# Second chunk of tokens: its second layer in split half precision instead of plain fp32, the weight splits and one batch's key preparation in other places

## Chip, cores, metric

One core of one Trainium2 chip. The metric is the device time of the program in microseconds (us); the time before is the median of three runs.

## What is computed

Attention over 4 batches, 8 heads, 576 positions and 64 columns per head, in which each row keeps only its 32 largest scores, and then two feed-forward layers over the 2304 tokens that come out.

```python
def _attn_ref(q, k, v):
    top_k = 32
    scores = scale * np.matmul(q, k.transpose(0, 1, 3, 2))
    kth = np.partition(scores, -top_k, axis=-1)[..., -top_k:-top_k + 1]
    scores = np.where(scores >= kth, scores, -1000000000.0)
    ...
    return np.matmul(attn, v).astype(np.float32)

def _moe_ref(x, w_gate, w_val, w_out):        # 512 -> 1536 -> 512
    gate = 1.0 / (1.0 + np.exp(-(x @ w_gate)))
    return (gate * (x @ w_val) @ w_out).astype(np.float32)

def _moe2_ref(x, w_in, w_out):                # 512 -> 2048 -> 512
    r = np.maximum(x @ w_in, 0.0)
    return (r * r @ w_out).astype(np.float32)
```

## The kernel before

**Tiles and chunks.** The 2304 tokens are 18 tiles of 128. They go through the kernel in 12 chunks: chunks 0 to 5 have one tile, chunks 6 to 11 two. For every chunk attention is computed first, in blocks: one block is one tile and one head, 128 rows by 576 scores. Chunks 0 to 5 have 8 blocks each (numbers 0 to 47 here), the others 16 each, 144 in all. In names a block is written as tile and head: `mx_2_1` is tile 2, head 1, which is block 17. A block takes, on VectorE (DVE), four `MAX8` (L389) and three `MATCH_REPLACE8` (L396) to find the 32nd largest score; ScalarE (ACT) copies scores out of PSUM and does the exponentials (L377, L408, L424), GpSimd (POOL) scales, TensorE (PE) multiplies queries by keys (`sp`, L374), turns the weights (`tp`, `tq`) and multiplies by the values (`xp`). Blocks go strictly one after the other on DVE, so the number of the block is the clock of the attention.

**The layers.** After a chunk's blocks come its two layers: `pg` and `pv` (gate and value, 6 pairs of column blocks), `acc1` (first layer's output), `ph` (8 pairs) and `acc2`. `th` (L759; `g`, L917, in the plain form) is the DVE product of gate and value that `acc1` waits for. There are two forms:

- **plain** (`moe32`, chunks 0 and 1): fp32 weights (`wg_c`, `wv_c`, `wo_c`, `wi_c`, `w2_c`) and fp32 activations.
- **split** (`moe`, chunks 2 to 11): weights and activations each as the sum of two fp16 numbers, high and low, and three fp16 products (`SPLIT`) for one fp32 product. The activations between the layers get a power-of-two scale from a sum of squares (`x2pq`, `x2cm`, `x2s`).

**The weights** come as 8-byte numbers through SyncE's queue (SP, L580). `conv` makes fp32 of them (ACT L607, L613, L616; DVE L609, L620; POOL L623); 34 pairs of blocks. `scale` finds a power-of-two scale for each weight matrix from its Gram matrix on PE (L640). `split` then makes the two fp16 parts of a pair: ACT L658 and DVE L661, or, for every third pair, POOL L663 and L664 in place of DVE. A pair's fp32 form can be given up only when the last plain chunk that needs it is through; the fp16 parts go into slots of the same pool of 35.

**Keys** of a batch are turned and cut into two parts by `prep_keys`, for two heads at a time: three loads (L152, L154), five PE transposes (L165), ACT copies (L172), DVE differences (L173), and four stores to DRAM (L179), which the loads `kst` (L326) read back. Batch 1 is first used in chunk 4.

**Order.** Program order on each engine is made before the run by a scheduler that walks the code with priorities. The loop at the end of the kernel sets them: in the plain part it gives attention blocks, conversion steps and layer steps due times (`ta`, `tw`, `tm`, with the steps `CA`, `CA2`, `CW`, `CM`), and `todo` holds the splits with the layer step after which each may come. From chunk 2 on, `attend` keeps attention a fixed number of blocks (`LEAD`, `LEAD2`) ahead of the layers. At run time each engine, SP's queue too, works through its own list strictly in that order.

Of the kernel before, what the change touches and what calls it, by code (L numbers as in the profile page):

```python
# [74 lines left out]
def tile_topk_attention__then__two_moe_layers(  # L75
# [692 lines left out]
    def moe(ci, nxt=None):  # L768

        m = ahead.pop(ci)  # L770
        tts, N, ix, l1_pair = chunks[ci], m.N, m.ix, m.l1_pair
        accs = []

        def l1_acc(fp, gh):
            if not accs:
                for h in range(2):
                    accs.append(ps_a.tile([P, 512], F32, tag="acc", name=f"acc1_{ci}_{h}"))

            last = fp == NF1 // 2 - 1
            for e, d in sorted(  # L780
                ((e, d) for e in range(2) for d in range(KM)),
                key=lambda t: (t[1], t[0]) if last else t,
            ):
                f = 2 * fp + e
                if True:
                    for x, (a, b_) in enumerate(SPLIT):
                        nc.tensor.matmul(  # L787
                            accs[d // 2][:, (d % 2) * N : (d % 2 + 1) * N],
                            wblk("wo", a, f, d * P, P),
                            gh[:, b_, e * N : (e + 1) * N],  # L790
                            start=(f == 0 and x == 0 and d % 2 == 0),
                            stop=(f == NF1 - 1 and x == 2),
                            skip_group_check=True,
                        )

        queue = m.queue
        depth = max(1, len(queue))
        for fp in range(len(queue), NF1 // 2):
            queue.append((fp, l1_pair(fp)))
            yield  # L800
            if len(queue) > depth:
                l1_acc(*queue.pop(0))
        while len(queue) > 1:
            l1_acc(*queue.pop(0))
        if nxt:
            nxt()
        l1_acc(*queue.pop(0))

        pool, kw = (wpool, {"tag": "w"}) if ci >= X2W else (mpool, {"tag": "m4", "bufs": M4})
        x2 = pool.tile([P, 2, KM, N], F16, name=f"x2_{ci}", **kw)  # L810
# [472 lines left out]
```

## Time and profile before

| | before |
|---|---|
| median of three runs (lowest to highest) | 1272.48 us (1272.18 to 1277.38) |
| profiled execution, its own time / its span | 1270.1 us / 1267.8 us |
| busy: PE, DVE, ACT, POOL | 1171.9, 956.3, 830.0, 844.9 us |
| share of the span | 92%, 75%, 65%, 67% |
| mean granted clock of TensorE | 0.966 |

The span runs from the first to the last instruction. Busy time is what the profiler saw each engine work; the rest of the span is idle time. The granted clock is the share of full speed that TensorE was allowed.

### The profile page before, as it was taken

What the parts mean: (1) busy time and instruction counts of PE and PEld (TensorE: products, weight loads), DVE (VectorE), ACT (ScalarE), POOL (GpSimd) and SP (SyncE); (2) the same over time, 40 slices, a digit from 0 to 9 for tenths busy, and PEclk for the clock granted to TensorE, in tenths of its full rate; (3) what the DMA queues carried; (4) which work ended last, traced back from release to release, by engine and by line L of the source; (5) the groups of instructions that cost most, each with busy time, mean ns of one, the idle gap of its engine ahead of it and who ended that gap; (6) DMA issues with size and microseconds to landing.
All of it is one profiled execution on the core that took longest, in us unless ns stands there. A gap on an engine that the chain in (4) does not pass through costs nothing.

```text
span 1267.8 us, 30670 instructions
## 1 busy us (share of the span) xinstructions
PE 1171.9 (92%) x11477; PEld 952.5 (75%) x11477; DVE 956.3 (75%) x1965; ACT 830.0 (65%) x1719; POOL 844.9 (67%) x1294
## 2 busy tenths in 40 slices
PE   6657889999889989899998999999999999999998
PEld 5436877987777868779786778877886887787775
DVE  6998789899789868889997788998999969210010
ACT  4998996577676766667766676776676757322122
POOL 1788774488776576777875887797688749515223
PEclk9667999999989999999997999999999999999999
DMA  6988763223354346665667465466544623200000
GB/s 183 366 293 284 259 191 85 57 78 88 109 151 118 95 93 147 147 134 119 146 128 155 99 164 120 119 138 154 105 101 92 126 48 67 55 1 1 18 1 17
DMA packets 243188, 153.92 MB, mean 121 GB/s; under 512 B 193120, under 2 KB 209504, under 8 KB 243040
## 3 DMA queue, kind: packets, MB, share of 16 engines
q1 hardware_dynamic: 243040, 151.97, 47.1%
q8 instruction: 90, 1.47, 0.5%
q14 instruction: 58, 0.48, 0.1%
HBM read 105.51 MB, written 18.09 MB: 97 GB/s over the span
## 4 chain that ended last, share of the span: by engine, by line
PE 62%; DVE 14%; ACT 9%; DMA 7%; POOL 5%; issue 3%; SPq 1%; DVEq 0%; POOLq 0%; ACTq 0%
PE ph L851 11%; PE acc L872 10%; PE pv L747 7%; PE pg L747 7%; PE acc L787 6%; PE sp L374 6%; DVE mx L389 5%; DVE W L396 5%; PE xp L506 2%; PE ph L952 2%; DMA PT<-S 2%; DMA kst<-ks 2%; PE acc L969 2%; PE xp L533 2%; PE qpt L334 1%
## 5 line engine op out<-in xcount | busy, mean ns | idle before, releaser
L389 DVE MAX8 mx<-W 128x8 f32<-128x576 f32 x432 | 327.9, 759 | 11.1
L396 DVE MATCH_REPLACE8 W<-mx,W 128x576 f32<-128x576 f32 x288 | 213.8, 742 | 0.0
L851 PE MATMUL ph<-x,wi_w 128*128 128x256 f16 (+1 forms) x1920 | 190.7, 252 | 4.6 <-ACT x L825 3.6
L872 PE MATMUL acc<-w_w,rh 128*128 128x512 f16 x768 | 181.8, 379 | 2.2 <-POOL rh L864 2.2
L851 PEld LDWEIGHTS <-wi_w 128*128 128x128 f16 x1920 | 156.4, 98 | 30.6 <-issue 5.2
L747 PE MATMUL pv<-xs,wv_w 128*128 128x256 f16 (+1 forms) x1440 | 147.0, 254 | 6.0 <-DVE th L759 4.8
L747 PE MATMUL pg<-xs,wg_w 128*128 128x256 f16 (+1 forms) x1440 | 148.2, 253 | 3.1 <-ACT xs L520 2.2
L374 PE MATMUL sp<-kst,qt 128*128 128x288 f32 x608 | 135.3, 335 | 15.7 <-DMA kst<-ks 8.8
L408 ACT ACTIVATE W<-S,mx 128x576 f32<-128x576 f32 x144 | 111.8, 776 | 51.7 <-DVE mx L389 51.4
L454 POOL TENSOR_TENSOR S<-W,S 128x512 f16<-128x512 f32 x192 | 137.0, 736 | 1.6
L747 PEld LDWEIGHTS <-wv_w 128*128 128x128 f16 x1440 | 117.9, 99 | 22.1 <-issue 9.2
L747 PEld LDWEIGHTS <-wg_w 128*128 128x128 f16 x1440 | 118.6, 99 | 17.4 <-issue 1.0
L377 ACT COPY S<-sp 128x576 f32<-128x576 f32 x144 | 92.0, 639 | 57.3 <-PE sp L374 37.5
L872 PEld LDWEIGHTS <-rh 128*128 128x128 f16 x768 | 72.5, 98 | 74.0 <-POOL rh L864 2.8
L787 PEld LDWEIGHTS <-wo_w 128*128 128x128 f16 x1440 | 117.9, 98 | 12.6 <-issue 0.8
L389 DVE MAX8 mx<-S 128x8 f32<-128x576 f32 x144 | 107.3, 745 | 25.0 <-ACT S L377 25.0
L759 DVE TENSOR_TENSOR th<-pv,th 128x512 f32<-128x512 f32 (+1 forms) x60 | 34.5, 576 | 121.3 <-PE pv L747 113.9
L374 PEld LDWEIGHTS sp<-kst,qt 128*128 128x128 f32 x608 | 92.4, 196 | 27.8 <-DMA kst<-ks 8.0
L452 POOL TENSOR_SCALAR W<-W,rz 128x576 f32<-128x576 f32 x96 | 71.9, 749 | 59.8 <-ACT S L451 57.4
L863 POOL TENSOR_TENSOR r<-r 128x512 f32<-128x512 f32 (+1 forms) x80 | 69.6, 871 | 57.4 <-ACT rh L862 51.8
L451 ACT ACTIVATE S<-W,rz 128x576 f16<-128x576 f32 x96 | 74.2, 774 | 50.4 <-DVE rz L447 47.1
L396 DVE MATCH_REPLACE8 W<-mx,S 128x576 f32<-128x576 f32 x144 | 106.9, 743 | 0.3 <-issue 0.3
(290 smaller groups left out, 2349.6 us busy)
## 6 DMA issues: line engine op xcount, KB each, us to landing
kst<-ks SPq DMA_DIRECT2D x112, 288.0 KB, 3.2
v<-vd SPq DMA_DIRECT2D x32, 320.0 KB, 3.4
qn<-in_q_dram SPq DMA_DIRECT2D x128, 64.0 KB, 2.4
wi_r<-in_moe_w_in_dram SPq DMA_DIRECT2D x16, 512.0 KB, 6.1
w_r<-in_moe_w_out_dram SPq DMA_DIRECT2D x16, 512.0 KB, 4.5
v<-in_v_dram SPq DMA_DIRECT2D x56, 128.0 KB, 2.4
wg_r<-in_moe_w_gate_dram SPq DMA_DIRECT2D x12, 512.0 KB, 6.4
wv_r<-in_moe_w_val_dram SPq DMA_DIRECT2D x12, 512.0 KB, 7.0
```

The lines of the kernel that those rows point to most:

```text
L374: nc.tensor.matmul(sp[:, e, 0:HALF], l, r, start=(x == 0), stop=(x == len(ops) - 1))
L377: nc.scalar.copy(ss.rearrange("p (e s) -> p e s", e=2), sp[:, :, 0:HALF])
L389: m8 = nc.vector.max(mx[:, r], cur)
L396: nc.vector.match_replace(wk, mx[:, r], cur, NEG)
L408: nc.scalar.activation(wk, ss, AF.Prelu, bias=kth, scale=-1.0, alpha=1.0 / BIG)
L451: nc.scalar.activation(pp[:, 0:S], wk, AF.Copy, scale=rz)
L452: nc.gpsimd.tensor_scalar(wk, wk, rz, 1.0, op0=ALU.mult, op1=ALU.mult)
L454: nc.gpsimd.tensor_tensor(pp[:, o : o + e - f], wk[:, f:e], pp[:, f:e], op=ALU.subtract)
L747: nc.tensor.matmul(pp[:, e * N : (e + 1) * N], wblk(wd, a, c, f0, P), xs[:, b_, c, :], start=(e == 0 and n == 0), stop=(n == 3 * KM - 1), ...
L787: nc.tensor.matmul(accs[d // 2][:, (d % 2) * N : (d % 2 + 1) * N], wblk("wo", a, f, d * P, P), gh[:, b_, e * N : (e + 1) * N], start=(f == ...
L851: nc.tensor.matmul(ph[:, e * N : (e + 1) * N], wblk("wi", a, c, f0, P), x2[:, b_, c, :], start=(e == 0 and n == 0), stop=(n == 3 * KM - 1) ...
L872: nc.tensor.matmul(acc2[i][:, 0:DM], gh[:, b_, e * N + i * P : e * N + (i + 1) * P], wblk("w2", a, f, 0, DM), start=(f == 0 and x == 0), s ...
```

## The change

Chunk 1 keeps its plain first layer, but its second layer is computed in the split form, by the same code as chunks 2 to 11 (moved out of `moe` into `second`). Since plain `wi` and `w2` are then last used in chunk 0, their splits come first: from the second half of chunk 0's steps on, with `wg`, `wv` and `wo` behind them during chunk 1. `wi` and `w2` get their Gram matrices at steps 7 and 11 in place of 9 and 13. Batch 1's keys are prepared during chunk 2's blocks (`KEYS1 = 2`), not chunk 1's. The plain form's `g` and `rr` are written over their inputs, and chunk 0's second layer keeps two pairs in flight, not one. Steps of chunk 1's second layer are set 3 apart in the due times, not 4.

```diff
-TD = 0
+MIXED = (1,)
+DEPTH1 = (1, 1)
+DEPTHP = 2
+CMS = 3.0
+W2S = 12
...
-KEYS1 = 1
-GRAM = {2: ("wg",), 3: ("wv",), 5: ("wo",), 9: ("wi",), 13: ("w2",)}
+KEYS1 = 2
+GRAM = {2: ("wg",), 3: ("wv",), 5: ("wo",), 7: ("wi",), 11: ("w2",)}
...
+    def second(ci, ix, x2, srcs, nxt=None):
+
+        tts = chunks[ci]
+        N = len(tts) * P
         KH = KM // 2
-        srcs = [a[:, 0 : KH * N].rearrange("p (d n) -> p d n", d=KH) for a in accs]
         with tc.high_priority(offset=XUP):
...
+        i2 = scales["w2"][1]
         us = mpool.tile([P, 2], F32, tag="us", bufs=2, name=f"us_{ci}")
-        nc.vector.scalar_tensor_tensor(us[:, 0:1], ix, iy, usc, op0=ALU.mult, op1=ALU.mult)
+        if ix is None:
+
+            nc.vector.scalar_tensor_tensor(
+                us[:, 0:1], iy, float(2.0 ** (2 * TB - 7)), scales["wi"][1], op0=ALU.mult, op1=ALU.mult
+            )
...
-            g = mpool.tile([P, 2 * N], F32, tag="hi", bufs=HIB, name=f"g_{ci}_{fp}")
-            nc.vector.tensor_tensor(g, pg[:, 2 * N : 4 * N], th, op=ALU.mult)
-            return g
+            nc.vector.tensor_tensor(th, pg[:, 2 * N : 4 * N], th, op=ALU.mult)
+            return th
...
+        if ci in MIXED:
+            x2 = xt.rearrange("p d n -> p (d n)").bitcast(F16)
+            h = KM * N // 2
+            yield from second(
+                ci,
+                None,
+                x2.rearrange("p (a c n) -> p a c n", a=2, c=KM),
+                [accs[0][:, i * h : (i + 1) * h].rearrange("p (d n) -> p d n", d=KM // 2) for i in range(2)],
+            )
+            return
...
+    ends = {n: (len(PLAIN) - 1) * per_chunk for n in ("wg", "wv", "wo")}
+    ends.update({n: (len(PLAIN) - 1 - len(MIXED)) * per_chunk for n in ("wi", "w2")})
     for i in range(len(pairs_of["wg"])):
-        todo.append((2 * (i // 2) + 2, "wg", i))
-        todo.append((2 * (i // 2) + 2, "wv", i))
+        todo.append((ends["wg"] + 2 * (i // 2) + 2, "wg", i))
+        todo.append((ends["wv"] + 2 * (i // 2) + 2, "wv", i))
...
-        todo.append((n1 + 2 * (i // 2) + 2, "wi", i))
+        todo.append((ends["wi"] + n1 + 2 * (i // 2) + 2, "wi", i))
     for i in range(len(pairs_of["w2"])):
-        todo.append((n1 + i + 3, "w2", i))
-    todo = [(max(t[0], TD), *t[1:]) for t in todo]
+        todo.append((ends["w2"] + max(n1 + i + 2 + DEPTHP, W2S), "w2", i))
...
-                tm += CM
-                if ci == PLAIN[-1]:
+                tm += CM if ci not in MIXED or n <= n1 else CMS
+                if nstep[0] == len(steps):
                     at(tm - SUP)
-                    while todo and todo[0][0] <= n:
+                    while todo and todo[0][0] <= PLAIN.index(ci) * per_chunk + n:
                         split(*todo.pop(0)[1:])
```

How the scheduler's lists move is seen at three places. (Lines of the changed kernel stand some 4 to 28 higher than in the kernel before.)

**SP's queue in chunk 1, before**, between two loads of keys for its heads 3 and 4 and the weight loads (`wi_r`):

```order
L326 DMA kst_1_3_0_994<-ks_0_1_145 128x576
L326 DMA kst_1_4_0_1082<-ks_0_2_245 128x576
L179 DMA ks_1_1_981<-kp_1_1_969 64x576 x2
L154 DMA ke_1_2_1350<-in_k_dram 64x2x64
L580 DMA wi_r2_2_1415<-in_moe2_w_in_dram 128x1024
L580 DMA wi_r3_2_1417<-in_moe2_w_in_dram 128x1024
L179 DMA ks_1_1_981<-kn_1_1_964 64x576 x2
L580 DMA wi_r0_3_1459<-in_moe2_w_in_dram 128x1024
```

The same place of the change, from the first of the two key loads:

```order
L330 DMA kst_1_3_0_949<-ks_0_1_145 128x576
L584 DMA wo_r4_0_748<-in_moe_w_out_dram 128x1024
L584 DMA wo_r5_0_750<-in_moe_w_out_dram 128x1024
L584 DMA wo_r6_0_808<-in_moe_w_out_dram 128x1024
L584 DMA wo_r7_0_810<-in_moe_w_out_dram 128x1024
L330 DMA kst_1_4_0_1036<-ks_0_2_245 128x576
L584 DMA wo_r8_0_822<-in_moe_w_out_dram 128x1024
```

Stores of batch 1's keys (`ks_1_1`), which wait for ACT and DVE, no longer stand ahead of weight loads; the queue has reached earlier weights (`wo_r`, not `wi_r`) when it comes to the keys of head 3.

**DVE in block 17, before** (tile 2, head 1): the scale of `wi` is worked out between the steps of the block.

```order
L389 MAX mx_2_1_2198<-S_2_1_2102 128x8
L646 TENSOR_TENSOR wi_d_2014<-wi_n_1948,ident_81 128x128
L396 MATCH_REPLACE W_2_1_2197<-mx_2_1_2198,S_2_1_2102 128x576
L389 MAX mx_2_1_2198<-W_2_1_2197 128x8
L429 RECIPROCAL rz_2_0_2151<-bs_2_0_2147 128x1
L396 MATCH_REPLACE W_2_1_2197<-mx_2_1_2198,W_2_1_2197 128x576
```

In the change (lines 4 higher) the same block holds the last conversion of `w2` and four splits of `wi`:

```order
L613 TENSOR_SCALAR w2_c7_1683<-w2_c7_1683 128x1024
L134 TENSOR_SCALAR wisn_1840<-wicx_1834 128x1
L137 TENSOR_SCALAR wis_1842<-wisn_1840 128x1
L140 TENSOR_SCALAR wis_1842<-wisn_1840 128x1
L1173 SCALAR_TENSOR_TENSOR usc_4630<-usc_4630,wis_1842 128x1
L665 SCALAR_TENSOR_TENSOR wi_w0_1857<-wi_c0_1026,wis_1842,wi_w0_1857 128x1024
L400 MATCH_REPLACE W_2_1_2245<-mx_2_1_2246,S_2_1_2036 128x576
L665 SCALAR_TENSOR_TENSOR wi_w1_1860<-wi_c1_1186,wis_1842,wi_w1_1860 128x1024
L393 MAX mx_2_1_2246<-W_2_1_2245 128x8
L400 MATCH_REPLACE W_2_1_2245<-mx_2_1_2246,W_2_1_2245 128x576
L665 SCALAR_TENSOR_TENSOR wi_w3_1949<-wi_c3_1349,wis_1842,wi_w3_1949 128x1024
```

Before, these `wi` splits stand in blocks 29 to 33.

**DVE in block 33, before** (tile 4, head 1), where the layers of chunk 2 run beside it (`th_2_2` is its product for pair 2):

```order
L661 SCALAR_TENSOR_TENSOR w2_w3_3263<-w2_c3_1707,w2s_2361,w2_w3_3263 128x1024
L396 MATCH_REPLACE W_4_1_3720<-mx_4_1_3721,S_4_1_3568 128x576
L389 MAX mx_4_1_3721<-W_4_1_3720 128x8
L661 SCALAR_TENSOR_TENSOR w2_w4_3330<-w2_c4_1719,w2s_2361,w2_w4_3330 128x1024
L396 MATCH_REPLACE W_4_1_3720<-mx_4_1_3721,W_4_1_3720 128x576
L759 TENSOR_TENSOR th_2_2_3970<-pv_2_2_3921,th_2_2_3970 128x256
```

The same block of the change:

```order
L400 MATCH_REPLACE W_4_1_3896<-mx_4_1_3897,S_4_1_3744 128x576
L393 MAX mx_4_1_3897<-W_4_1_3896 128x8
L400 MATCH_REPLACE W_4_1_3896<-mx_4_1_3897,W_4_1_3896 128x576
L393 MAX mx_4_1_3897<-W_4_1_3896 128x8
L763 TENSOR_TENSOR th_2_3_4227<-pv_2_3_4178,th_2_3_4227 128x256
L400 MATCH_REPLACE W_4_1_3896<-mx_4_1_3897,W_4_1_3896 128x576
```

The splits are gone from here, and chunk 2 is one pair further.

## Rows read from the trace of the kernel before

**Rows 1.** Stretches: us, busy PE, PEld, DVE, ACT, POOL, clock, DMA, GB/s.

```profile
84.30:193.50 109.20, 87.77 (x713) 76.10 (x714) 90.81 (x171) 99.83 (x180) 86.02 (x83) 0.87 0.76 246
193.50:252.50 59.00, 59.00 (x522) 50.52 (x521) 51.30 (x107) 34.13 (x72) 25.24 (x48) 1.00 0.25 70
252.50:314.20 61.70, 59.84 (x479) 50.10 (x477) 58.94 (x107) 48.54 (x94) 49.58 (x65) 1.00 0.30 83
314.20:388.60 74.40, 65.63 (x864) 58.41 (x862) 61.00 (x127) 53.84 (x127) 56.64 (x96) 0.93 0.45 126
388.60:435.90 47.30, 47.30 (x644) 40.99 (x641) 45.23 (x99) 33.66 (x80) 26.55 (x57) 1.00 0.36 98
435.90:563.70 127.80, 112.50 (x1520) 93.18 (x1518) 99.77 (x231) 86.50 (x211) 92.74 (x170) 1.00 0.58 131
563.70:1085.00 521.30, 510.34 (x5094) 407.42 (x5092) 467.59 (x979) 361.77 (x762) 400.85 (x663) 0.99 0.54 117
1085.00:1267.80 182.80, 176.40 (x1433) 135.94 (x1431) 12.67 (x28) 45.12 (x75) 59.88 (x64) 1.00 0.05 14
...
365.00:370.00 5.00, 4.27 (x27) 3.78 (x26) 4.93 (x13) 2.59 (x6) 3.78 (x8) 0.51 0.80 224
```

**Rows 2.** The same stages for L389 alone: us, DVE busy (instructions), clock, DMA.

```profile
193.50:252.50 59.00, 23.63 (x33) 1.00 0.25 70
563.70:1085.00 521.30, 236.30 (x321) 0.99 0.54 117
```

**Rows 3.** Chain that ended last, in order of time: start, us, what, records.

```profile
283.64 1.78 PE ph L952 x16
285.43 1.72 PE acc L969 x4
372.16 1.56 PE ph L851 x28
1156.80 2.59 PE acc L872 x12
```

**Rows 4.** Groups by form: line, names, shapes, count | busy us, mean ns | idle.

```profile
L661 DVE SCALAR_TENSOR_TENSOR w_w<-w_c,w2s,w_w 128x1024 f16<-128x1024 f32 x5 | 10.1, 2020 | 0.9 <-ACT w_w L658 0.9
L661 DVE SCALAR_TENSOR_TENSOR wi_w<-wi_c,wis,wi_w 128x1024 f16<-128x1024 f32 x6 | 8.6, 1435 | 0.1
L609 DVE TENSOR_SCALAR w_c<-w_c 128x1024 uint32<-128x1024 uint32 x8 | 6.6, 829 | 6.4 <-ACT w_c L607 6.4
L173 DVE TENSOR_TENSOR kn<-kpt,kp 128x512 fp32r<-128x512 f32 x12 | 8.2, 682 | 2.8 <-ACT kp L172 2.8
L172 ACT CAST kp<-kpt 128x512 fp32r<-128x512 f32 x16 | 9.5, 591 | 7.0 <-PE kpt L165 6.9
L607 ACT ACTIVATE w_c<-w_r 128x512 f32<-128x512 f32 x16 | 10.2, 677 | 0.4 <-POOL w_c L623 0.4
L826 DVE SCALAR_TENSOR_TENSOR x<-acc,x2s,x 128x256 f16<-128x256 f32 x8 | 3.6, 472 | 0.1
L864 POOL TENSOR_TENSOR rh<-r,rh 128x256 f16<-128x256 f32 x32 | 21.4, 673 | 0.7
```

**Rows 5.** Waits, SP 84 to 194 us, DVE 0 to 390: us, times, longest.

```profile
SPq L179 <- ACT kp L172: 8.8, 3, 5.6
...
DVE w_c L609 <- ACT w_c L607: 6.4, 3, 3.7
DVE wi_c L609 <- ACT wi_c L607: 6.3, 2, 4.4
```

**Rows 6.** Timeline of PE and DVE, 332 to 344 us.

```profile
332.10 1.50 PE L747 MATMUL pv<-xs,wv_w 128*128 128x128 f16 x24
332.85 4.37 DVE L661 SCALAR_TENSOR_TENSOR w_w<-w_c,w2s,w_w 128x1024 f16<-128x1024 f32 x1
341.04 2.57 PE L747 MATMUL pv<-xs,wv_w 128*128 128x128 f16 x24 [4.75 <-DVE th L759]
```

**Rows 7.** Chain that ended last, shares by line, 436 to 564 us.

```profile
by line: DMA PT<-S 13.7%; DVE mx L389 10.8%; DVE W L396 9.0%; DMA kst<-ks 8.2%; PE ph L851 7.9%; PE sp L374 5.7%; issue 5.0%; PE acc L872 4.9%; PE pg L747 3.3%; DMA vd<-vom 3.2%; PE pv L747 3.2%; PE acc L787 2.6%; SPq L298 2.5%; DMA kn<-in_
```

More of the change, by code (lines that the diff above doesn't have):

```diff
@@ L766, in moe_head @@
         m.N, m.ix, m.l1_pair = N, ix, l1_pair
[L768 to L810, printed above, removed]
+    def second(ci, ix, x2, srcs, nxt=None):
+        tts = chunks[ci]
+        N = len(tts) * P
         KH = KM // 2
-        srcs = [a[:, 0 : KH * N].rearrange("p (d n) -> p d n", d=KH) for a in accs]
         with tc.high_priority(offset=XUP):
@@ L892, in moe, with l1_acc @@
         yield
+    def moe(ci, nxt=None):
+        m = ahead.pop(ci)
+        tts, N, ix, l1_pair = chunks[ci], m.N, m.ix, m.l1_pair
+        accs = []
+        def l1_acc(fp, gh):
+            if not accs:
+                for h in range(2):
+                    accs.append(ps_a.tile([P, 512], F32, tag="acc", name=f"acc1_{ci}_{h}"))
+            last = fp == NF1 // 2 - 1
+            for e, d in sorted(
+                ((e, d) for e in range(2) for d in range(KM)),
+                key=lambda t: (t[1], t[0]) if last else t,
+            ):
+                f = 2 * fp + e
+                if True:
+                    for x, (a, b_) in enumerate(SPLIT):
+                        nc.tensor.matmul(
+                            accs[d // 2][:, (d % 2) * N : (d % 2 + 1) * N],
+                            wblk("wo", a, f, d * P, P),
+                            gh[:, b_, e * N : (e + 1) * N],
+                            start=(f == 0 and x == 0 and d % 2 == 0),
+                            stop=(f == NF1 - 1 and x == 2),
+                            skip_group_check=True,
+                        )
+        queue = m.queue
+        depth = max(1, len(queue))
+        for fp in range(len(queue), NF1 // 2):
+            queue.append((fp, l1_pair(fp)))
+            yield
+            if len(queue) > depth:
+                l1_acc(*queue.pop(0))
+        while len(queue) > 1:
+            l1_acc(*queue.pop(0))
+        if nxt:
+            nxt()
+        l1_acc(*queue.pop(0))
+        pool, kw = (wpool, {"tag": "w"}) if ci >= X2W else (mpool, {"tag": "m4", "bufs": M4})
+        x2 = pool.tile([P, 2, KM, N], F16, name=f"x2_{ci}", **kw)
+        KH = KM // 2
+        srcs = [a[:, 0 : KH * N].rearrange("p (d n) -> p d n", d=KH) for a in accs]
+        yield from second(ci, ix, x2, srcs, nxt)
     def moe32(ci, xt):
@@ L961, in l2_pair @@
             nc.scalar.activation(r, ph[:, 0 : 2 * N], AF.Relu)
-            g = mpool.tile([P, 2 * N], F32, tag="hi", bufs=HIB, name=f"rr_{ci}_{fp}")
-            nc.gpsimd.tensor_tensor(g, r, r, op=ALU.mult)
-            return g
+            nc.gpsimd.tensor_tensor(r, r, r, op=ALU.mult)
+            return r
         def l2_acc(fp, g):
@@ L975, in l2_acc @@
                 )
-        prev = None
+        prev = []
         for fp in range(NF2 // 2):
-            g = l2_pair(fp)
+            prev.append((fp, l2_pair(fp)))
             yield
-            if prev is not None:
-                l2_acc(*prev)
-            prev = (fp, g)
-        l2_acc(*prev)
+            if len(prev) > DEPTHP:
+                l2_acc(*prev.pop(0))
+        for p in prev:
+            l2_acc(*p)
         tt = chunks[ci][0]
@@ L1149, in layer2_scales @@
             usc.append(u)
-        return usc[0], scales["w2"][1]
+        return usc[0]
     att = attention()
```

19 lines of the change are left out of this document (11 added, 8 removed).

## Prediction

> **What bounds the kernel now.** I read first the table of stretches, cut where DVE begins blocks 8, 16, 24, 32, 40, 48, 64 and where its last block ends [rows 1]. The row of L389 shows that a cut is right: 33 `MAX8` in the second stretch are 8 blocks of 4, and one more at the edge [rows 2]. Four kinds of stage stand out. In blocks 8 to 15 ACT is busy 99.8 of 109.2 us: it converts weights. In blocks 16 to 31 PE is busy 118.8 of 120.7 us and DVE 110.2. In blocks 32 to 39 nobody is full (PE 65.6 of 74.4). In blocks 48 to 63 PE idles 15 us, and the chain of waits there runs through DMA (`PT`, `kst`) and DVE's L389 and L396, with little PE in it [rows 7]. After that PE is busy 98% until block 143 ends, and then 183 us of layers are left that PE does alone [rows 1]. So the end is set by how early the attention gets through the first 64 blocks, and from there on by PE's work.
>
> The profiled execution took 1270.1 us; the median of the runs is 2.4 above it. The sum is made against 1270.1, and 2.4 is added. A measurement of this kernel can tell some 0.5% from no change, 6.4 us.
>
> **What is removed and added.** Plain second layer of chunk 1: a `ph` pair is 16 records, 8 products at 0.222 each, in 1.78 us, an `acc` pair 4 records, 2 products at 0.86, in 1.72 [rows 3]; 8 of each, 28.0 us. In the split form it is 192 fp16 products of 128 columns at 1.56/28 = 0.056 us and 48 of 512 columns at 2.59/12 = 0.216 [rows 3], 10.7 + 10.4, and 4 for `x2pq`, 21.3. PE saves 6.7 us. DVE gets two halves of L826 at 0.47 [rows 4] and a handful of one-column steps, 2 us; POOL 8 operations of 0.67 [rows 4], 5.4, and ACT as many of about the same size. POOL and ACT are idle 12 and 13 of the 62 us of that stage [rows 1], which hides them; bare, in a chain of 8 pairs, they would cost up to 5.
>
> **What is moved.** I counted by the lists of both kernels what stands between the same blocks on DVE and PE, and priced it by rows. One price is open: a DVE split cost 2.02 us in the mean for `w2` and 1.44 for `wi` [rows 4]. I take 1.6, nearer the lower, since 6 against 5 splits are of it and the rest is between.
>
> *Blocks 0 to 15.* DVE loses 4 key preparations (0.68 and a short end each, 3.6 us), 4 conversion pairs of `w2` (0.83 and sign steps, 6 in all), 2 splits (3.2), one gate product: 13. PE loses 52 plain products at 0.222 and 2 at 0.86, 13 us, and 20 transposes, which I price like plain products, 4. ACT, which bounds this stage, loses 8 conversions at 0.68, 3 more of that size, 2 of twice the size, 4 key copies at 0.59 and their ends [rows 4], 2 splits: 15.8 in all. At its present share of 91%, 84.0 us of ACT take 92. That is -17 us. The least gain: DVE's 13 alone, less what it now waits, -10. The most: SP's stores waited 8.8 us for the key copies, with weight loads behind them in the queue, and DVE waited 12.7 us for conversions [rows 5]; half of that gone makes -24.
>
> *Blocks 16 to 23.* Here it is paid back. DVE gets 17 more splits (27), the 4 key preparations (3.6), 4 conversion pairs (6) and 3 gate products: 38 on top of 51.3, 89.3. PE gets 97 more plain products at 0.222, 2 at 0.86, and the transposes: 27 on top of 59.0, 86. DVE is the fuller one. In blocks 24 to 31, where both were full, it was busy 95.5% [rows 1]; at that share 89.3 us take 93.5: +34.5. The least loss: PE alone at its 97%, 88.7, +29.7. The most: all 20 splits at 2.02 and the conversions dearer too, +46.
>
> *Blocks 24 to 31.* 8 splits fewer, 2 us more for the new layer: DVE 58.9 becomes 47. PE: 130 plain products at 0.222 and 10 at 0.86 give way to 30, 202 fp16 ones at 0.056 and 42 at 0.216; 59.8 becomes 49.6, which at 97% take 51.1: -10.6. Between -12 and -6.
>
> *Blocks 32 to 39.* 7 splits leave. One of them took 4.37 us, the gate product `th` stood behind it on DVE, PE waited 4.75 us for `th`, and its next 24 products took 2.57 us where 24 before had taken 1.50 [rows 6]. The granted clock later fell to half once more (0.51 in 365 to 370) [rows 1]. The stage's mean clock of 0.93 means that some 10 of its 74.4 us ran at half (1.2 GHz); half of that, less what was idle, makes 4.5 of PE's 65.6 us. By count 5.2 us more of products come in. 66.3 us at 97% are 68.4: -6. Between -9 (no wait at all) and 0 (a wait of the same kind comes back elsewhere in the stage).
>
> *Blocks 40 to 47.* PE loses 3.4 of 47.3, but DVE gets 2 of chunk 3's layer work on 45.2; 47.5 at 95.5% are 49.8: +2.5 (-1 to +3).
>
> *Blocks 48 to 63.* PE has 3.9 us less. The chain there is little PE's [rows 7], so half comes through: -2 (0 to -4).
>
> *Blocks 64 on.* 4.5 us less for PE by count, at 98% busy: -4 (-2.5 to -4.5). After block 143 the lists hold the same work, 0.
>
> Sum: -17 + 34.5 - 10.6 - 6 + 2.5 - 2 - 4 = -2.6, so 1267.5, and 1270 as a median. The saved 6.7 us of PE are mostly given back as idle time of PE in the dense stage (93.5 against 86).
>
> **A rule against the change.** The two `w_w` and `wi_w` rows show the same DVE instruction at 2020 and 1435 ns [rows 4], and a single one at 4.37 us [rows 6]. The Trainium skill, SBUF — State Buffer, section "SBUF: two separate sides", says that DVE and GpSimd share one pair of ports by an exclusive lock, and that a DVE operation with two SBUF inputs and a GpSimd operation that reads SBUF keep each other out for a whole instruction. The two durations agree with it, though no row names the lock. By this rule 20 DVE splits in one stage, with POOL's own splits beside them, would nearly all pay the higher price; that is the slower rival below.
>
> **The rivals.**
>
> *Faster: SP's queue and DVE's waits were dearer than the work.* For it: 12.7 us of DVE waits for conversions, 8.8 us of SP behind key copies [rows 5]. Against it: ACT was 91% busy, so there is little to regain beyond its own work. Blocks 0 to 15 give -24, the dense stage runs at PE's pace, +29.7, the rest as above: -14.4, median 1258. It decides if DVE's busy time in the dense stage stays under some 84 us. Chance 0.32.
>
> *Slower: DVE and POOL hold each other up in the dense stage.* 20 splits at 2.02 instead of 1.6 are +8, conversions and gate products behind them +3 to +4; chunk 1's first layer waits for these gate products as chunk 2's did, and PE's clock falls to half in such a gap. +46 in place of +34.5, and 1.5 for half clock: +10.4, median 1283. It decides where splits there average over 1.9 us. Chance 0.20.
>
> *No effect of the new layer.* It is cheaper by PE, but if blocks 24 to 47 are set by DVE and the chain of ACT and POOL, none of 6.7 us arrives: -2.6 + 6 = +3.4, median 1276. For it: DVE was 95.5% busy in 24 to 31. Against: DVE loses 12 us there too. Chance 0.10.
>
> **How the numbers follow.** My forecast, about no change, 0.36, with a range of its own from 1264 to 1277; with the last rival some 0.44 within 0.5%. The faster rival and the lower edge of the forecast: 0.34 under 1266. The slower one and its edge: 0.22 over 1279. Likeliest 1270. All better ends together give -24.8, all worse ones +30.5 (medians 1248 and 1303), but they are of different stages and will not come together; half way from the sum to either is 1259 and 1286. I take the lower edge to 1255, so that the faster rival lies within: 1255 to 1286 for 8 in 10.
>
> **What would show it.** In the changed profile: block 16 begins near 177 us (193.5 before); blocks 16 to 23 take 90 to 98 us with DVE over 93% busy; L661 averages 1.5 to 1.7 us; block 32 begins within 8 us of 314 + 7; the wait of `pv` for `th` and the half clock near 341 us are gone; PE's busy time falls by 6 to 11 us; blocks 64 to 143 and the tail take as long as before within 5 us. I am wrong if block 16 does not come at least 10 us earlier, if blocks 16 to 23 take under 88 or over 104 us, or if the stretch of blocks 48 to 63 moves by more than 5 us: it holds waits for DMA that I take to be fixed, and chunks 3 to 5, which now begin up to 3 blocks earlier, could fill or widen them.

## The result

| | before | changed |
|---|---|---|
| median of five runs | 1273.06 us | 1293.06 us (1288.33 to 1295.08) |
| profiled execution / its span | 1270.1 / 1267.8 us | 1290.21 / 1288.4 us |
| mean granted clock of TensorE | 0.966 | 0.954 |

The changed kernel is slower: ratio 1.0147, 95% interval 1.0126 to 1.0168. The forecast was 1270, between 1255 and 1286.

The first line of the page after, with which the spans can be taken apart (busy time, share, instructions):

```profile
PE 1177.9 (91%) x11561; PEld 956.3 (74%) x11561; DVE 958.1 (74%) x1973; ACT 832.4 (65%) x1730; POOL 853.6 (66%) x1302
```

PE's busy time was to fall by 6 to 11 us and rose by 6.0 (1171.9 before). The span grew by 20.6; so PE's idle time grew by 14.6, from 95.9 to 110.5. By the prediction's count 6.7 us of products fell away, so the rest ran some 12.7 us slower than before; that the granted clock is the reason is an estimate: busy time by mean granted clock gives 1132 us before and 1124 now, but the profiles of the kernel before further down, which hold the same products, give 1125 to 1152 by it. The lower clock is to be seen in the stretches. They are cut as in [rows 1] at blocks 8, 16, 24, 32, 40, 48 and 64, and then every 16 blocks; the line after the tail is blocks 64 to 143 together.

```profile
80.80:170.00 89.20, 72.41 (x584) 63.68 (x581) 85.68 (x155) 86.74 (x158) 74.59 (x72) 0.85 0.70 237
170.00:274.10 104.10, 96.08 (x802) 82.28 (x801) 87.22 (x142) 73.70 (x125) 78.23 (x78) 0.97 0.38 101
274.10:326.90 52.80, 46.04 (x471) 36.18 (x469) 49.06 (x106) 38.90 (x92) 36.27 (x65) 0.97 0.32 90
326.90:401.90 75.00, 70.43 (x940) 61.47 (x939) 48.07 (x120) 45.19 (x121) 44.90 (x93) 0.95 0.45 126
401.90:450.90 49.00, 46.77 (x665) 42.54 (x663) 47.36 (x109) 34.70 (x84) 25.78 (x56) 0.97 0.35 95
450.90:572.70 121.80, 110.45 (x1486) 92.94 (x1485) 95.70 (x225) 83.43 (x202) 91.09 (x169) 0.97 0.61 135
572.70:677.80 105.10, 94.69 (x1039) 78.28 (x1037) 93.20 (x198) 69.31 (x153) 73.26 (x128) 0.97 0.55 122
677.80:801.20 123.40, 110.52 (x989) 85.48 (x988) 94.70 (x208) 80.97 (x177) 89.79 (x147) 0.94 0.60 134
1105.70:1288.40 182.70, 176.36 (x1433) 135.93 (x1430) 12.48 (x27) 44.79 (x75) 59.69 (x64) 1.00 0.05 14
572.70:1105.70 533.00, 507.55 (x4974) 402.11 (x4972) 466.51 (x977) 361.03 (x760) 398.18 (x659) 0.98 0.52 114
```

Two things are to be seen. First, the dense stage (blocks 16 to 23) takes 104.1 us where 59.0 stood: PE is busy 96.1 us in it (59.0 before) and idles 8.0 (0.0 before), at a clock of 0.97. Second, blocks 64 to 143, forecast 4 us shorter, take 533.0 in place of 521.3, and PE's idle time there grows by more than that: 25.5 us against 11.0 [rows 1].

**What happens in the dense stage.** DVE, then ACT, then PE, around 229 us (start, duration, engine, line, in brackets the wait before it):

```profile
227.47 0.68 DVE L177 TENSOR_TENSOR kn<-kpt,kp 128x512 fp32r<-128x512 f32 x1
...
228.79 3.03 DVE L665 SCALAR_TENSOR_TENSOR w_w<-w_c,w2s,w_w 128x1024 f16<-128x1024 f32 x1
...
233.07 1.26 DVE L665 SCALAR_TENSOR_TENSOR w_w<-w_c,w2s,w_w 128x1024 f16<-128x1024 f32 x1
...
234.99 1.27 DVE L665 SCALAR_TENSOR_TENSOR wv_w<-wv_c,wvs,wv_w 128x1024 f16<-128x1024 f32 x1
...
236.91 1.26 DVE L665 SCALAR_TENSOR_TENSOR wg_w<-wg_c,wgs,wg_w 128x1024 f16<-128x1024 f32 x1
...
238.83 0.21 DVE L177 TENSOR_TENSOR kn<-kpt,kp 128x64 fp32r<-128x64 f32 x1
```

```profile
231.85 1.15 ACT L662 ACTIVATE wg_w<-wg_c,wgs 128x1024 f16<-128x1024 f32 x1 [2.60 <-DVE w_w L665]
...
235.37 1.13 ACT L662 ACTIVATE wg_w<-wg_c,wgs 128x1024 f16<-128x1024 f32 x1
...
236.88 0.20 ACT L176 CAST kp<-kpt 128x64 fp32r<-128x64 f32 x1
```

```profile
230.02 0.27 PE L169 MATMUL kpt<-ident,ke 64*128 64x64 f32 x1
...
233.01 1.95 PE L924 MATMUL pg<-x_plain,wv_c 128*128 128x128 f32 x16
239.09 1.11 PE L478 MATMUL tp<-ident,W 128*128 128x128 f32 x4 [4.13 <-DVE kn L177]
241.00 3.78 PE L945 MATMUL acc<-th,wo_c 128*128 128x128 f32 x16 [0.80 <-DVE th L935]
```

PE has turned the last piece of a key (`kpt`) by 230.3 us. DVE's difference `kn`, which reads it out of PSUM, comes only at 238.83; on DVE four splits, 6.8 us, lie between. But `kn` also needs ACT's copy `kp`, and that ends only at 237.08: ACT had waited 2.60 us for DVE's long split and then worked off its own halves of splits (L662) and the block's steps. From there the last split and one step of the block on DVE hold `kn` for 1.75 us more. So splits delay it on both engines. PE's next transposes `tp` wait 4.13 us for it. Then 16 products take 3.78 us, where 16 of the same shape took 1.95 just before. The three stretches of 5 us from 235 on show the granted clock (third number from the end) fall to half and come back:

```profile
235.00:240.00 5.00, 0.91 (x4) 0.71 (x4) 4.70 (x9) 4.09 (x8) 3.70 (x4) 0.80 0.39 111
240.00:245.00 5.00, 4.20 (x20) 4.00 (x20) 4.47 (x7) 3.57 (x6) 5.00 (x5) 0.51 0.27 62
245.00:250.00 5.00, 5.00 (x47) 5.00 (x47) 4.15 (x8) 3.52 (x8) 5.00 (x5) 1.00 0.00 0
```

**What happens late.** PE's waits in blocks 64 to 79 (total, times, longest), and its timeline at block 64:

```profile
PE xp L510 <- DMA PT<-S: 5.7, 3, 2.6
PE kpt L169 <- DMA kn<-in_k_dram: 2.8, 1, 2.8
```

```profile
572.07 0.83 PE L751 MATMUL pv<-xs,wv_w 128*128 128x128 f16 x12
...
575.72 1.47 PE L510 MATMUL xp<-PT,v 128*64 128x128 f16 x27 [2.64 <-DMA PT<-S]
577.11 1.33 PE L378 MATMUL sp<-kst,qt 128*128 128x288 f32 x4
578.24 1.38 PE L751 MATMUL pv<-xs,wv_w 128*128 128x128 f16 x12
```

The wait for `PT` in the same stretch before the change:

```profile
PE xp L506 <- DMA PT<-S: 1.3, 1, 1.3
```

PE has come to `xp` in its list 2.64 us ahead of the transposed weights `PT`, which a DMA brings. The 12 products of `pv` behind it take 1.38 us, 0.83 before the gap. The waits for `PT` in this stretch come to 5.7 us, 1.3 before the change.

### The profile page after: what moved, and what is told of

Its sections match the earlier page's. It is cut to its first block, busy times and chain, and to the rows that moved or that the text cites. A ratio compares the mean times of both kernels' runs of the same rounds, so it can differ in the third digit from the quotient of the medians.

```text
span 1288.4 us, 30890 instructions
## 1 busy us (share of the span) xinstructions
PE 1177.9 (91%) x11561; PEld 956.3 (74%) x11561; DVE 958.1 (74%) x1973; ACT 832.4 (65%) x1730; POOL 853.6 (66%) x1302
## 4 chain that ended last, share of the span: by engine, by line
PE 52%; DVE 14%; DMA 10%; POOL 8%; ACT 8%; issue 4%; SPq 2%; POOLq 0%; DVEq 0%; ACTq 0%
PE ph L823 10%; PE acc L844 10%; DVE mx L393 6%; PE acc L885 6%; PE pg L751 6%; PE pv L751 6%; DVE W L400 5%; PE sp L378 4%; DMA PT<-S 3%; PE xp L510 2%; DMA kst<-ks 2%; PE xp L537 2%; POOL S L458 1%; PE acc L945 1%; DMA kn<-in_k_dram 1%
## 5 line engine op out<-in xcount | busy, mean ns | idle before, releaser
L823 PE MATMUL ph<-x,wi_w 128*128 128x256 f16 (+1 forms) x1920 | 193.6, 256 | 7.5 <-ACT x L789 7.1
L823 PEld LDWEIGHTS <-wi_w 128*128 128x128 f16 x2112 | 172.5, 101 | 36.0 <-issue 9.4
L844 PE MATMUL acc<-w_w,rh 128*128 128x512 f16 x816 | 193.5, 379 | 0.1
L751 PE MATMUL pg<-xs,wg_w 128*128 128x256 f16 (+1 forms) x1440 | 150.9, 254 | 3.0 <-ACT xs L524 2.1
L751 PE MATMUL pv<-xs,wv_w 128*128 128x256 f16 (+1 forms) x1440 | 143.9, 252 | 2.4 <-DVE th L763 1.4
L844 PEld LDWEIGHTS <-rh 128*128 128x128 f16 x816 | 77.0, 98 | 76.3 <-POOL rh L836 0.4
L885 PEld LDWEIGHTS <-wo_w 128*128 128x128 f16 x1440 | 117.8, 98 | 13.8 <-issue 1.1
L763 DVE TENSOR_TENSOR th<-pv,th 128x512 f32<-128x512 f32 (+1 forms) x60 | 34.5, 575 | 121.0 <-PE pv L751 117.1
L835 POOL TENSOR_TENSOR r<-r 128x512 f32<-128x512 f32 (+1 forms) x88 | 74.4, 845 | 63.4 <-ACT rh L834 62.4
L885 PE MATMUL acc<-gh,wo_w 128*128 128x256 f16 (+1 forms) x1104 | 106.1, 249 | 0.0
```

The costliest lines, as they stand in the source:

```text
L751: nc.tensor.matmul(pp[:, e * N : (e + 1) * N], wblk(wd, a, c, f0, P), xs[:, b_, c, :], start=(e == 0 and n == 0), stop=(n == 3 * KM - 1), ...
L823: nc.tensor.matmul(ph[:, e * N : (e + 1) * N], wblk("wi", a, c, f0, P), x2[:, b_, c, :], start=(e == 0 and n == 0), stop=(n == 3 * KM - 1) ...
L835: nc.gpsimd.tensor_tensor(r, r, r, op=ALU.mult)
L844: nc.tensor.matmul(acc2[i][:, 0:DM], gh[:, b_, e * N + i * P : e * N + (i + 1) * P], wblk("w2", a, f, 0, DM), start=(f == 0 and x == 0), s ...
L885: nc.tensor.matmul(accs[d // 2][:, (d % 2) * N : (d % 2 + 1) * N], wblk("wo", a, f, d * P, P), gh[:, b_, e * N : (e + 1) * N], start=(f == ...
```

## The experiments

The theory after the result: the splits and the moved keys, packed into blocks 16 to 24, delay on DVE what PE waits for, and the long gaps are followed by half clock. Three rivals: the keys alone are the harm; POOL's splits and DVE's hold each other up; or much of the 20 us is chance of the order, since the scheduler's list is made anew by any edit. Block starts below are the first `MAX8` of a block on DVE.

**One part alone, or taken back.** The first is an edit of the kernel before, the others of the changed one.

```diff
-KEYS1 = 1          # b_keys2
+KEYS1 = 2
-KEYS1 = 2          # a_keys1
+KEYS1 = 1
-MIXED = (1,)       # a_plain2
+MIXED = ()
-LOP = 3            # a_lop0
+LOP = 0
```

> The kernel before with only batch 1's keys prepared during chunk 2's blocks. Packing theory (the harm comes from the weight splits pressed into blocks 16 to 23, the keys are a small part): blocks 8 to 15 gain 4 to 10 us, blocks 16 to 23 lose 4 to 8, the time stays within 6 us of 1273. Rival (the moved keys are the harm: their DVE differences hold PSUM buffers that the attention's transposes need): blocks 16 to 23 lose over 12, 1283 or more.

> The changed kernel with batch 1's keys back in chunk 1's blocks. Packing theory: blocks 8 to 15 take 6 to 12 us longer than the change's 89.2, blocks 16 to 23 take 94 to 100 in place of 104.1, the time is 1286 to 1296, the late stages stay as long as in the change. Rival of the keys: blocks 16 to 23 under 92, time under 1280.

> The changed kernel with chunk 1's second layer plain again, so that the splits of w_in and w_out2 also go back behind that layer's steps; keys, Gram steps and the depth of chunk 0's layer stay as changed. Packing theory: blocks 16 to 23 fall from 104 to 64 to 72, blocks 24 to 39 get back to 136 to 142, and the late stages fall back to the kernel before: 1268 to 1278. Rival (the late loss of some 12 us comes from the scheduler's new order as such, not from the packing): blocks 64 to 143 stay 8 us or more above the 521 of before, 1280 to 1290.

> The changed kernel with no split on POOL: all of them on DVE. If DVE's own work is what fills blocks 16 to 24 (no lock between DVE and POOL): L665 stays at 1.6 to 1.7 us a split, DVE gets 6 to 8 more of them there, 10 to 13 us, blocks 16 to 23 take 106 to 116, time 1293 to 1305. If DVE and POOL hold each other up: L665 falls under 1.45 us, blocks 16 to 23 take 104 or less, time 1290 or less.

| | ratio to before (95%) | blocks 8-15 | 16-23 | block 64 starts | 64-143 to the last block's start |
|---|---|---|---|---|---|
| before | 1 | 109.3 | 58.9 | 563.7 | 515.4 |
| changed | 1.0147 (1.0126-1.0168) | 89.2 | 104.1 | 572.7 | 527.1 |
| b_keys2 | 1.0049 (1.0026-1.0072) | 87.4 | 89.8 | 569.9 | 518.6 |
| a_keys1 | 1.0062 (1.0035-1.0089) | 106.8 | 80.4 | 568.0 | 520.3 |
| a_plain2 | 1.0121 (1.0095-1.0147) | 88.3 | 93.5 | 582.8 | 515.9 |
| a_lop0 | 1.0044 (1.0025-1.0063) | 88.2 | 110.8 | 567.3 | 518.3 |

The move of the keys alone shortens blocks 8 to 15 by 22 us and lengthens 16 to 23 by 31, far more than the packing case of b_keys2 had; only its time came in (1278.96, within 6 us of 1273). In a_keys1 both signs of the keys' rival came: blocks 16 to 23 at 80.4 us and 1279.73. But these shifts of the blocks are no price of keys. In blocks 8 to 15 of b_keys2 PE does 609 instructions, before 713, in blocks 16 to 23 747, before 522: the attention's blocks come earlier against the layers and conversions, and the work that they passed comes back a stage later. Where a block starts does not say how much of the layers is done; only the ends count.

In a_keys1, with the keys away, the gap in the dense stage is there all the same, by another door. The gate product's way over ACT, POOL and DVE, and PE's wait:

```profile
244.41 1.15 ACT L662 ACTIVATE wv_w<-wv_c,wvs 128x1024 f16<-128x1024 f32 x1 [2.63 <-POOL wi_w L668]
245.93 0.39 ACT L933 ACTIVATE th<-pg 128x256 f32<-128x256 f32 x1
247.64 0.40 POOL L934 TENSOR_SCALAR th<-th 128x256 f32<-128x256 f32 x1
248.15 3.06 DVE L665 SCALAR_TENSOR_TENSOR wg_w<-wg_c,wgs,wg_w 128x1024 f16<-128x1024 f32 x1
```

```profile
251.60 3.78 PE L945 MATMUL acc<-th,wo_c 128*128 128x128 f32 x16 [7.28 <-DVE th L935]
```

The gate product `th` comes late on ACT, behind a half split that had waited 2.63 us for POOL's; on DVE it then stands behind a split of 3.06 us. PE waits 7.28 us in all, and again 16 products take 3.78 us. So the keys are not the harm by themselves. a_plain2 missed both of its cases: blocks 16 to 23 take 93.5 us, not 64 to 72, there is no late loss (515.9), and it is slow all the same (1288.85), by what it loses up to block 64. Whether the late loss was chance stayed open.

a_lop0 contradicts its first expectation (1293 to 1305): 1279.75. Its splits are shorter (count, busy us, mean ns), ahead of them those of the changed kernel:

```profile
L665 DVE SCALAR_TENSOR_TENSOR w_w<-w_c,w2s,w_w 128x1024 f16<-128x1024 f32 x6 | 13.5, 2253 | 1.2 <-ACT w_w L662 1.2
L665 DVE SCALAR_TENSOR_TENSOR wi_w<-wi_c,wis,wi_w 128x1024 f16<-128x1024 f32 x5 | 8.7, 1743 | 1.4 <-ACT wi_w L662 1.4
```

```profile
L665 DVE SCALAR_TENSOR_TENSOR wi_w<-wi_c,wis,wi_w 128x1024 f16<-128x1024 f32 x8 | 12.0, 1524 | 1.4 <-ACT wi_w L662 1.4
L665 DVE SCALAR_TENSOR_TENSOR w_w<-w_c,w2s,w_w 128x1024 f16<-128x1024 f32 x8 | 10.7, 1356 | 1.2 <-ACT w_w L662 1.2
```

All 34 splits on DVE take 46.2 us, 1.36 each; 23 with POOL's beside them had taken 38.3, 1.66 each. So that rival has its mechanism and its time (1290 or less), but not its place: blocks 16 to 23, which now hold all 34, take 110.8 us, not 104 or less, as the other case had it (106 to 116).

**Edits without content.** To see how much chance there is, due times were changed by under 0.7%, with no work added, removed or moved on purpose. Four such edits of each kernel:

```diff
-CM = 4.0           # b_null; a_null, there CMS = 3.02 too
+CM = 4.02
-CA2 = 5.0          # b_null_ca2, a_null_ca2
+CA2 = 4.98
-CA = 6.0           # b_null_ca, a_null_ca
+CA = 5.98
-MUP = 200.0        # b_null_mup, a_null_mup
+MUP = 201.0
```

> The kernel before with the due-time step of the plain layers at 4.02 in place of 4.00: no work added, removed or moved on purpose, only ties in the scheduler's order fall otherwise. If the differences between the variants have causes in what they move: 1273 within 3 us. Rival (chance of the order: any edit shifts the lists, and the late stages answer with some us of idle time either way): it moves by 5 us or more.

> The changed kernel with the due-time steps of the plain layers at 4.02 and 3.02 in place of 4.00 and 3.00, a like edit without content. Causes: 1293 within 3 us, with blocks 64 to 143 again 8 us or more over the 515 of before. Rival (chance of the order): the late loss shrinks by half or more, and the time is 1280 to 1288.

> The kernel before with the due-time step of the attention blocks from the 16th on at 4.98 in place of 5.00, a second edit without content (the first made the kernel before 9 us slower). If the kernel before is one low draw among the orders that the scheduler can give: 1278 to 1290. If the first one was an exception: 1270 to 1277.

> The kernel before with the due-time step of the first attention blocks at 5.98 in place of 6.00, a third edit without content. A low draw: 1278 to 1290. An exception: 1270 to 1277.

> The changed kernel with the same step at 4.98. Its order differs little up to block 40 (147 of DVE's rows). If the late loss of 11.7 us in blocks 64 to 143 is a high draw: it falls under 6 us, time 1278 to 1288. If it comes from what was changed: 1290 to 1296.

> The changed kernel with the step of the first attention blocks at 5.98. A high draw: 1276 to 1288, late loss under 6 us. From what was changed: 1290 to 1296.

> The kernel before with the lead of the plain layers' steps at 201 in place of 200, a fourth edit without content. If the two groups of orders stay apart by 0.5%: ratio 1.002 to 1.008. If they are one: over 1.009.

> The changed kernel with the same lead at 201. Groups apart: ratio 1.006 to 1.013, PE idle 7 to 10 us in blocks 16 to 23 once more. One group: under 1.005.

| | ratio (95%) | block 16 starts | 16-23 | 24-63 | 64-143 | span |
|---|---|---|---|---|---|---|
| before | 1 | 193.6 | 58.9 | 311.2 | 515.4 | 1267.8 |
| b_null | 1.0074 (1.0050-1.0098) | 191.8 | 65.5 | 319.9 | 515.9 | 1281.8 |
| b_null_ca2 | 1.0043 (1.0023-1.0063) | 194.2 | 58.9 | 319.3 | 515.9 | 1278.8 |
| b_null_ca | 1.0040 (1.0014-1.0067) | 191.9 | 65.5 | 306.4 | 528.2 | 1280.6 |
| b_null_mup | 1.0024 (1.0008-1.0040) | 190.3 | 63.0 | 311.2 | 521.3 | 1276.0 |
| changed | 1.0147 (1.0126-1.0168) | 170.0 | 104.1 | 298.5 | 527.1 | 1288.4 |
| a_null | 1.0065 (1.0040-1.0089) | 168.0 | 105.8 | 301.0 | 517.8 | 1282.9 |
| a_null_ca2 | 1.0101 (1.0077-1.0125) | 169.7 | 103.8 | 301.4 | 524.8 | 1290.1 |
| a_null_ca | 1.0056 (1.0036-1.0075) | 168.3 | 107.6 | 301.2 | 517.1 | 1282.9 |
| a_null_mup | 1.0056 (1.0029-1.0082) | 171.0 | 102.4 | 296.7 | 521.9 | 1282.3 |

Each ratio is to the kernel before on the same chip. Two of the eight edits changed no order at all: in the traces a_null_ca2 runs the very list of the changed kernel, and a_null_ca that of a_null. On every engine and in SP's queue each instruction stands in the same place, by line, names (without buffer numbers), shape and semaphores. So the kernel before is seen in five lists and the changed one in three, two of them twice.

The repeats tell how far one list comes back. Blocks 64 to 143 repeat within 2.3 us (527.1 and 524.8; 517.8 and 517.1). The ratio repeats within 0.1 points for the one list (1.0065, 1.0056), but reads 1.0147 and then 1.0101 for the other. There the changed kernel's medians agree (1293.06 and 1292.95); it is the kernel before that stood at 1273.06 in the first measurement and at 1276.88 in the later one.

Chance of the order is large. The four other lists of the kernel before are slower than it by 0.24 to 0.74%, and the two other lists of the changed kernel are faster than it, at 1.0061 and 1.0056, in the midst of those four. The expectations of a_null, a_null_ca and the four of before came out for chance, or within their first case; a_null_ca2 came out for a cause, as a repeat of the same list must, and a_null_mup (1.0056) fell between its two cases. The late stretch goes with the list too, but its length is no measure of loss: b_null_ca, a kernel without the change, takes 528.2 us there and a_null 517.8, yet PE idles less in b_null_ca. Two stretches each (blocks 64 to 79 and 80 to 95), first of a_null, then of b_null_ca (idle PE 14.9 and 12.9 us together):

```profile
574.70:672.70 98.00, 92.65 (x1032) 77.21 (x1030) 92.82 (x197) 68.68 (x152) 72.43 (x127) 0.98 0.59 129
672.70:795.60 122.90, 113.37 (x1010) 87.26 (x1009) 94.92 (x209) 80.89 (x177) 89.99 (x147) 0.93 0.58 134
```

```profile
563.70:667.50 103.80, 97.50 (x1161) 81.30 (x1158) 93.02 (x199) 71.58 (x159) 74.98 (x133) 0.98 0.61 130
667.50:791.70 124.20, 117.60 (x1079) 91.83 (x1078) 98.85 (x211) 81.59 (x179) 91.85 (x150) 0.99 0.58 132
```

From block 64 to the start of the last block PE is idle 11.0 to 19.0 us in the five lists of before (mean 15.1), 25.4 and 24.5 in the two runs of the changed list, and 18.4 to 19.1 in its other two lists.

What does not go with chance: in blocks 16 to 23 PE is idle 7.4 to 9.7 us in all five profiles of the changed kernel and 0.0 in all five of the kernel before. Over the whole span (span less PE's busy time) it is idle 95.6 to 104.7 us before and 108.1 to 115.8 changed. The time is less clear. The mean ratio is 1.0036 for the five lists of before (standard deviation 0.0027) and 1.0080 for the three of the change (0.0038; a list that ran twice counts by its mean). Their difference, 0.44%, has a standard error of 0.25% (0.0027²/5 + 0.0038²/3, and the root of it): not clear of zero. So the 1.47% divide into 0.36 by which the kernel before lies under the mean of its lists, 0.44 between the two means, and 0.67 by which the first measurement of the changed kernel lies over the mean of its own; 0.23 of the last is no order, since the same list gives 1.0124 in the mean of its two measurements.

**What packing costs, and undoing it.** The first lets the splits of `wg`, `wv` and `wo` come 4 layer steps later in the changed kernel. The next four take both edits back that had helped alone (keys in chunk 1's blocks, no splits on POOL), under four settings. The last is the kernel before without splits on POOL.

```diff
-    ends = {n: (len(PLAIN) - 1) * per_chunk for n in ("wg", "wv", "wo")}       # a_late_splits
+    ends = {n: (len(PLAIN) - 1) * per_chunk + 4 for n in ("wg", "wv", "wo")}
...
-KEYS1 = 2          # c_keys1_lop0; c_k1l0_null, _mup and _ca with the edits of a_null, a_null_mup, a_null_ca too
+KEYS1 = 1
-LOP = 3            # c_keys1_lop0 and its orders; b_lop0, there alone
+LOP = 0
```

> The changed kernel with the splits of w_gate, w_val and w_out allowed 4 layer steps later, so that fewer stand in blocks 20 to 23 and more behind. If packing makes PE idle: idle plus half clock in blocks 16 to 23 falls from 8 + 2.4 us to under 6 together, and comes back in part in blocks 24 to 31. If something else does (the keys, the split layer): it stays at 8 or more. The time may fall anywhere between 1278 and 1293, by the late stages.

> The changed kernel with both single edits that made it faster: batch 1's keys back in chunk 1's blocks (1279.7 alone), and no split on POOL (1279.8 alone). If they have different causes (transposes and copies of the keys on PE and ACT; splits on POOL beside DVE's), the gains add: 1264 to 1269, PE idle and half clock in blocks 16 to 40 down to some 15 us. If it is one cause (too much work in blocks 16 to 24, or the chance of the order): 1275 to 1281.

> Keys back and no splits on POOL (ratio 1.0026), with the due-time steps at 4.02 and 3.02. If these two undo most of the change's own loss: ratio 0.998 to 1.006. If 1.0026 was a lucky order: 1.007 to 1.013.

> Keys back and no splits on POOL, third order (lead of the plain steps 201). If the undoing gets back what packing costs: ratio 0.999 to 1.006, idle PE in blocks 16 to 23 at 4 us or less. If not: 1.007 to 1.012 with 7 us or more of idle PE there.

> Keys back and no splits on POOL, fourth order (first attention blocks 5.98 apart). The same two cases: 0.999 to 1.006 with 4 us or less of idle PE in blocks 16 to 23, or 1.007 to 1.012 with 7 us or more.

> The kernel before with no split on POOL: control for the last one. If POOL's splits hurt only where splits are packed together, as in the change: DVE, 95.5% busy in blocks 24 to 31 before, gets 11 more splits of 1.4 us, and the time is 1275 to 1285. If POOL's splits cost everywhere (a DVE split beside one of POOL's takes 2.0 to 2.3 us, alone 1.3): 1262 to 1270.

Blocks 16 to 23 of a_plain2 and of c_k1l0_null, and the splits on DVE (line L665 alone: busy, count, clock) in these blocks of the changed kernel, of a_late_splits and of c_k1l0_null:

```profile
170.30:263.80 93.50, 90.80 (x778) 77.58 (x777) 69.37 (x130) 56.41 (x108) 49.97 (x65) 1.00 0.42 116
```

```profile
193.10:275.00 81.90, 81.88 (x708) 71.14 (x705) 80.39 (x134) 64.17 (x107) 36.03 (x53) 1.00 0.23 61
```

```profile
170.00:274.10 104.10, 34.43 (x20) 0.97 0.38 101
```

```profile
169.80:275.10 105.30, 38.13 (x20) 0.97 0.36 98
```

```profile
193.10:275.00 81.90, 38.04 (x29) 1.00 0.23 61
```

a_late_splits (1.0094, 1.0067 to 1.0120) did not thin the stage: it holds 20 splits as before, and PE idles 8.6 us. So it tells nothing on packing, though by its expectation 8 us or more spoke against it. a_plain2 has 8 splits there, and 2.7 us of idle PE are left. But packing alone is not the cause either: c_k1l0_null has 29 splits on DVE in these blocks, DVE is busy 80.4 of 81.9 us, and PE never idles. The four runs with keys and POOL's splits taken back have 3.6, 0.0, 2.6 and 0.0 us of idle PE there; taken back alone, the keys leave 7.6 (a_keys1) and POOL's splits 9.5 (a_lop0). What is left of the theory is narrower: the splits make gaps where they are long (1.72 us in the mean here, 1.31 in c_k1l0_null) or where keys wait behind them; that fits the lists shown, but was not tested by itself, and length alone does not do it: a_null has 1.55 us and idles 8.5.

And the time does not follow the gaps: the four runs (three lists; those of c_k1l0_null and c_k1l0_ca are the same but for four of PE's records) measure 1.0026 (1.0010 to 1.0043), 1.0072 (1.0043 to 1.0101), 1.0113 (1.0089 to 1.0138) and 1.0071 (1.0042 to 1.0100), mean 1.0070, which is neither the 1.0036 nor the 1.0080. In c_k1l0_mup and c_k1l0_ca the idle time came out for the case that the undoing helps and the ratio for the case that it does not; c_k1l0_null came out for the lucky order. c_k1l0_mup, with 2.6 us of idle PE in the dense stage, idles 13.1 and 14.1 in blocks 64 to 79 and 80 to 95. That the two gains would add to 1264 to 1269 was wrong: c_keys1_lop0 took 1278.83, the size named for one cause or for chance. Whether the undoing gets back the change's own cost stays undecided. b_lop0 (1.0065, 1.0044 to 1.0086) came out inside its first case. No version beat the kernel before.

## Why the prediction was wrong

The sum, beside the two profiles and beside the means of the five profiles of each kernel (differences of the table above; the tail is what follows the start of the last block):

| step of the prediction | forecast | the two profiles | means of five profiles |
|---|---|---|---|
| blocks 0 to 15 | -17 | -23.6 | -23.0 |
| blocks 16 to 23 | +34.5 | +45.2 | +42.4 |
| blocks 24 to 63 (-10.6, -6, +2.5, -2) | -16.1 | -12.7 | -13.8 |
| blocks 64 on | -4 | +11.7 | +2.4 |
| tail | 0 | 0.0 | +0.3 |
| sum | -2.6 | +20.6 | +8.3 |

- **"Blocks 64 on: -4" failed first and most, by 15.7 us.** It took for given that PE stays 98% busy there and that less work must be less time. The work did fall (5094 to 4974 records, 510.3 to 507.6 us busy), but idle PE rose by 14.5. By the edits without content more than half of this is the draw: the kernel before idles 11.0 us there in its own list and 15.1 in the mean of its five, the changed one 25 in its own and 20.9 in the mean of its three. I had taken the 521.3 us of [rows 1] as a property of the kernel; it belongs to one order of it.
- **Blocks 16 to 23, +34.5, was too small by 10.7, some 8 in the mean, and the term that was mis-sized is PE's work.** DVE's was right: 87.2 us busy, forecast 89.3. So was the idle time of PE: 93.5 against 86 left 7.5, and it idles 8.0. But PE is busy 96.1 us, not 86, so PE is the fuller engine there (92%, DVE 84%), not DVE, and neither is the bound alone. Of the 10 us some 2.4 are half clock (the stage's clock is 0.97). 3.3 are `xp` of attention, which the count did not have (100 records in place of 60), 1.7 two `acc` products more than counted, and the rest is spread over small groups. The plain products are as counted, some 96 for 97. The two stages for `xp` alone (PE, PEld and ACT busy):

```profile
193.50:252.50 59.00, 4.38 (x60) 3.14 (x60) 0.96 (x4) 1.00 0.25 70
170.00:274.10 104.10, 7.72 (x100) 5.42 (x100) 1.33 (x5) 0.97 0.38 101
```

  The idle time came by a way that the forecast did not have. It was to come from a full DVE; it came from waits for `kn` and `th` (4.1 and 2.1 of the 8.0 us), which splits delay on DVE and ACT. I had the wait for the gate products in the text, but only in the slower rival, and the keys' not at all. That part of the sum was right by luck. With 104.1 us the stage lies just past the 104 that I had set as a bound.
- **Blocks 0 to 15, -17, came out at -23.6**, the end that I had named as the most (-24; half of both waits that I named, 8.8 and 12.7 us, would have made it -28). What is pushed out of one stretch of blocks comes back in the next: up to block 24 the forecast was +17.5, the profiles say +21.6, the means +19.4; this sum was off by 2 to 4, less than its parts.
- **Blocks 32 to 39, -6, came out at +0.6.** The wait of `pv` for `th` [rows 6] is gone, but the other end that I had named came: PE waits 3.3 us in its place, `ph` for the scaled activations `x` of ACT, and the stage's clock is 0.95. Blocks 48 to 63 gained 6.0, not 2, just over the 5 that I had set as a bound.
- **The new layer's 6.7 us** are saved by count alone; PE's busy time, which was to fall by 6 to 11, rose by 6.0 between the two profiles and fell by 3 between the means of the lists (1177.3 to 1174.4), while idle PE rose by 14.6 and 11.
- **The rivals.** The faster one was wrong. The slower one named the size (+46), the half clock and a mechanism that is there (the split of 3.03 us), but not at the strength that it set: splits of over 1.9 us in the mean did not come (34.4 us for 20 in blocks 16 to 23, 1.72). Against the 1.6 that I took, that adds 2.4 us of DVE. That the new layer has no effect could not be told apart: a_plain2 without it (1.0121) is no faster than the mean of the changed kernel's lists.
- **The range** was made from bounds of prices alone. A term for the order itself, by the runs 0.27 to 0.38% (3.5 to 5 us) as one standard deviation for each kernel, was missing. Added in squares to the half width it moves the upper edge only to some 1288 (an estimate), so 1293 would still have lain outside. What the change is worth apart from its order is 0.44%, with twice the standard error -0.1 to 0.9%: by my own sizes between no difference and slower.

Open is which wait of the many starts the late draw: `PT` and the keys of the next batch are the ones that PE meets, but what in the order moves them was not found. That chance of the order explains the 0.36 rests on four other lists; for the 0.67 it rests on two other lists and one repeat, no more.

## What to carry to other kernels

Where a scheduler makes the order, an edit without content is the first control: here it moves the time by up to 0.7%, as much as most of the edits with content, so one order tells little under 1%. Look in the trace whether such an edit changed the order at all: two of eight here did not, and are repeats, not new draws. When work is packed beside a full engine, look at what stands behind it in the queue of every engine that takes a part of it, and look for every gap of the waiting engine whether the clock fell after it. A cut by attention's blocks tells how far attention is, not how much of the rest is done: check a stretch that became shorter by the instructions that it held.
